# Top-32 attention and a hard-swish feed-forward: a shorter softmax chain, one reciprocal for two halves, and key/query transposes moved from TensorE to the DMA crossbar

## The chip, the cores and the metric

The kernel runs on one core of a Trainium2 chip, in one launch. The metric is the device time in microseconds. The kernel before takes 1581.81 us, the median of three runs (1580.72 to 1583.69). The execution that the profile shows took 1580.33 us and has a span of 1578.5 us from its first to its last instruction.

The core has five engines that run their own instruction streams, each strictly in the order in which the program wrote it, and wait for one another by semaphores: TensorE (PE in the profile, with its weight loads as PEld), VectorE (DVE), ScalarE (ACT), GpSimd (POOL) and SyncE (SP), which here issues the DMAs.

## What is computed

There are 8 batches with 8 heads, 576 queries and keys of 64 elements. In every row of 576 scores only the 32 largest are kept; their softmax weights the values. The result, 4608 tokens of 512, goes through a feed-forward layer of 2048 with a hard-swish gate.

```python
scores = scale * np.matmul(q, k.transpose(0, 1, 3, 2))
kth = np.partition(scores, -32, axis=-1)[..., -32:-31]
scores = np.where(scores >= kth, scores, -1e9)
attn = np.exp(scores - np.max(scores, axis=-1, keepdims=True))
attn = attn / (np.sum(attn, axis=-1, keepdims=True) + 1e-09)
x = np.matmul(attn, v)            # then (B,H,S,D) -> (B*S, H*D)
h = x @ w_in                      # 512 -> 2048
out = (h * np.clip(h + 3.0, 0.0, 6.0) / 6.0) @ w_out
```

## The kernel before

The words of the program: a **pair** is two heads of one batch, a **duo** is one tile of 128 queries of two pairs. In a duo each pair is one half (u = 0 or 1) with two rows of 576 scores per partition, one row for each head. The 64 queries that are left over from 576 = 4 x 128 + 64 make **leftover duos** (`rest`): both heads share the 128 partitions, and a half has one row only. There are 80 duos, 16 of them leftover.

The program is written as a sequence of **slots**, eight to a duo. In each slot VectorE gets one of the four rounds that find the 32 largest scores of a half:

```python
def top(self, u, r):                       # round r of half u
    ...
    for t in range(self.nt):               # nt = 2 rows, or 1 in a leftover duo
        nc.vector.max(self.m[u][:, t, 8*r : 8*r+8], self.cur[t])        # the 8 largest
    if r < TOP_K // 8 - 1:
        for t in range(self.nt):
            nc.vector.match_replace(wk, self.m[u][...], self.cur[t], LOWEST)
```

What follows for a half is a chain over the other engines:

```python
def shift(self, u):        # GpSimd: (32nd largest - largest) * scale
    nc.gpsimd.tensor_tensor(d[:, 0:nt], m[:, 0:nt, TOP_K-1], m[:, 0:nt, 0], ALU.subtract)
    nc.gpsimd.tensor_scalar_mul(d[:, 0:nt], d[:, 0:nt], scale)
def exp(self, u):          # ScalarE: Prelu, then Exp with the row's sum, then + EPS
    ... AF.Prelu, bias=m[:, t, TOP_K-1:TOP_K] ...
    ... AF.Exp, bias=self.less[u][:, t:t+1], accum_out=self.den[:, u, t:t+1] ...
    nc.scalar.activation(d, d, AF.Copy, bias=EPS)
def inverse(self, u):      # VectorE
    nc.vector.reciprocal(d, d)
def weights(self, u):      # GpSimd: times 1/sum, then the two 16-bit halves of each word apart
    ...
def flip(self, u):         # the DMA crossbar transposes the 16-bit halves
    nc.sync.dma_start_transpose(t16[:, 0:n, :], self.e16[u][:, 0 : n * P])
def join(self, u):         # halves together again: ScalarE for u = 0, GpSimd for u = 1
    ...
def values(self, dst):     # TensorE: weights times values;  place(): ScalarE copies the result
    ...
```

When each part is queued is a table of slots, counted from the duo's first slot; so 8 is the first slot of the next duo:

```python
usual = dict(
    shift0=3, exp0=4, inverse0=9, weights0=10, flip0=12, join0=15,
    shift1=7, exp1=8, inverse1=13, weights1=14, flip1=16, join1=19, values=22, place=23,
)
behind = dict(usual, values=25, place=26)      # second to next-to-last part of the run
```

After `place` of two full duos a **block** of 128 tokens goes to the feed-forward queue. A block has 16 **pieces**: eight make h = x @ w_in (a piece is 16 TensorE instructions of 128 columns), eight add h's gate times w_out into `acc` (4 instructions of 512 columns). Slots take about one piece each; a leftover duo's slots take half of that:

```python
due += ((left > 0) + (left >= 24) / 8 + (left >= 48) / 8) / (2 if u and u.rest else 1)
piece(int(due))
```

Keys and queries come as rows of 64 and are transposed on TensorE, nine instructions for a pair, and copied from PSUM by ScalarE:

```python
def transpose(self):
    ps = big()
    for j in range(2 * J + 1):
        rows = self.landed[:, j, :, :].rearrange("p h d -> p (h d)")
        nc.tensor.transpose(ps[:, j * P : (j + 1) * P], rows, ident[:])
    nc.scalar.copy(kq[:, 0:c0], ps[:, 0:c0])
    ...                                        # three smaller copies
```

The scores of the next duo are made in slot 1 (TensorE) and copied by ScalarE in the same slot. In the first duos the 64-bit weights are also turned into 32-bit words (`convert`: 32 chunks, ScalarE, GpSimd, then two VectorE instructions, lines 117 and 118, then GpSimd).

Of the kernel before, what the change touches and what calls it, by code (L numbers as in the profile page):

```python
# [29 lines left out]
def kernel(  # L30
# [65 lines left out]
    def convert(dst, src):  # L96

        st = kqpool.tile([P, 2 * WC], U32, tag="kq", name="st")
        nc.sync.dma_start(st[:], src)
        yield
        words = st[:].rearrange("p (n two) -> p n two", two=2)
        lo, hi = words[:, :, 0], words[:, :, 1]
        a = gpool.tile([P, WC], F32, tag="g", name="a")
        y = gpool.tile([P, WC], F32, tag="g", name="y")
        nc.scalar.activation(a[:], hi.bitcast(F32), AF.Abs)
        nc.gpsimd.tensor_scalar(a[:], a[:], HI_MOST, HI_LEAST, ALU.min, ALU.max)

        nc.scalar.activation(y[:], lo, AF.Copy, bias=2.0, scale=2.0**-51)
        yield

        au, yu = a[:].bitcast(U32), y[:].bitcast(U32)
        nc.vector.tensor_scalar(au, au, 3, None, ALU.logical_shift_left)  # L117
        nc.vector.scalar_tensor_tensor(  # L118
            out=yu, in0=hi, scalar=0x80000000, in1=yu,
            op0=ALU.bitwise_and, op1=ALU.bitwise_or,  # L120
        )
        yield
        nc.gpsimd.tensor_tensor(
            dst.bitcast(I32), a[:].bitcast(I32), y[:].bitcast(I32), ALU.add
        )
# [13 lines left out]
    class Pair:  # L139
# [6 lines left out]
        def load(self):  # L146
            h0 = 2 * self.hp
            t = self.landed = kqpool.tile([P, 2 * J + 1, 2, D], F32, tag="kq", name="landed")
            for i, src in enumerate((k, q)):
                for hh in range(2):  # L150
                    nc.sync.dma_start(
                        t[:, i * J : (i + 1) * J, hh, :],
                        src[self.b, h0 + hh, 0:JP, :].rearrange("(p j) d -> p j d", j=J),
                    )
                nc.sync.dma_start(
                    t[i * R : (i + 1) * R, 2 * J, :, :],
                    src[self.b, h0 : h0 + 2, JP:S, :].rearrange("h s d -> s h d"),
                )
# [12 lines left out]
        def transpose(self):  # L171
            kq = kqpool.tile([P, JP + S], F32, tag="kq", name="kq")
            self.kT, self.qT = kq[:, 0:JP], kq[:, JP : JP + S]
            ps = big()
            for j in range(2 * J + 1):
                rows = self.landed[:, j, :, :].rearrange("p h d -> p (h d)")
                nc.tensor.transpose(ps[:, j * P : (j + 1) * P], rows, ident[:])  # L177
            c0 = 2 * JP
            nc.scalar.copy(kq[:, 0:c0], ps[:, 0:c0])
            nc.scalar.copy(kq[:, c0 : c0 + R], ps[:, c0 + R : c0 + 2 * R])  # L180
            for hh in range(2):
                d = slice(hh * D, (hh + 1) * D)
                nc.scalar.copy(self.kr[d, hh, :], ps[d, c0 : c0 + R])

    class Duo:
# [14 lines left out]
        def scores(self, us=(0, 1)):  # L200

            if us[0] == 0:
                self.sc = scpool.tile([P, 2, 2 * (S + R)], F32, tag="sc", name="sc")
                self.den = mpool.tile([P, 2, 2], F32, tag="den", name="den")
            sc, nu = self.sc[:, us[0] : us[-1] + 1, :], len(us)
            ps = big()
# [4 lines left out]
            if self.rest:  # L211
                for i, u in enumerate(us):
                    pr = self.pairs[u]
                    for d in heads:
                        nc.tensor.matmul(banks[d, i, :], pr.qT[d, qs], pr.kT[d, :])
                    for hh, d in enumerate(heads):
                        nc.tensor.matmul(left[d, i * R : (i + 1) * R], pr.qT[d, qs], pr.kr[d, hh, :])
                nc.gpsimd.memset(sc[:, :, S : S + R], 0.0)
                nc.scalar.copy(sc[:, :, 0:JP], banks[:, 0:nu, :])
                nc.scalar.copy(  # L220
                    sc[:, :, JP:S], left[:, 0 : nu * R].rearrange("p (u r) -> p u r", r=R)
                )
                return
# [5 lines left out]
            for i, u in enumerate(us):  # L229
                pr = self.pairs[u]  # L230
                for hh, d in enumerate(heads):
                    nc.tensor.matmul(banks[:, 2 * i + hh, :], pr.qT[d, qs], pr.kT[d, :])  # L232
            nc.scalar.copy(  # L233
# [25 lines left out]
        def shift(self, u):  # L259

            nt, m = self.nt, self.m[u]
            d = self.less[u] = mpool.tile([P, 2], F32, tag="shift", name="shift")
            nc.gpsimd.tensor_tensor(
                d[:, 0:nt], m[:, 0:nt, TOP_K - 1], m[:, 0:nt, 0], ALU.subtract
            )
            nc.gpsimd.tensor_scalar_mul(d[:, 0:nt], d[:, 0:nt], scale)  # L266

        def exp(self, u):
# [7 lines left out]
            for t in range(nt):  # L276
                row = self.row(u, t)
                nc.scalar.activation(  # L278
                    row, row, AF.Exp, bias=self.less[u][:, t : t + 1], scale=-scale / FLAT,
                    accum_out=self.den[:, u, t : t + 1],  # L280
                )
            d = self.den[:, u, 0:nt]
            nc.scalar.activation(d, d, AF.Copy, bias=EPS)

        def inverse(self, u):
            d = self.den[:, u, 0 : self.nt]
            nc.vector.reciprocal(d, d)  # L287
# [64 lines left out]
    def feed_forward(xT, rows):  # L352
# [6 lines left out]
        for f0 in range(0, NFC, nf):  # L359
# [12 lines left out]
            g = gpool.tile([P, 512], F32, tag="g", name="g")  # L372
            nc.scalar.activation(g[:], h[:], AF.Relu, bias=three[:], scale=1.0)  # L373
            hs = hpool.tile([P, 512], F32, tag="h", name="hs")
            nc.scalar.copy(hs[:], h[:])
            gs.append(g)

            def gate(g=g, hs=hs):
                nc.gpsimd.tensor_scalar(g[:], g[:], 6.0, 0.0, ALU.min, ALU.max)  # L379
                nc.gpsimd.tensor_tensor(g[:], g[:], hs[:], ALU.mult)  # L380

            yield gate
        acc = ps_w.tile([P, DM], F32, tag="w", name="acc")
        for f in range(NFC):
# [7 lines left out]
            if f % 2 == 1:  # L392
                if f == NFC - 1:
                    o = opool.tile([P, DM], F32, tag="o", name="o")
                    nc.scalar.mul(o[:], acc[:], 1.0 / 6.0)  # L395
                    for p0, p1, dst in rows:
                        nc.sync.dma_start(dst, o[p0:p1, :])
                yield None

# [5 lines left out]
    for b in range(B):  # L405
        halves = [pairs[b][0:2], pairs[b][2:4]]
        for qt in range(J):
# [3 lines left out]
            if qt == (0 if b == B - 1 else J - 1) and not 2 < b < B - 1:  # L411
# [11 lines left out]
    gates = []  # L423

    def piece(count=1):
        nonlocal left
        for _ in range(count):
            while todo:
                try:
                    gates.append(next(todo[0]))  # L430
                    left -= 1
                    break
                except StopIteration:
                    todo.pop(0)
            else:
                gates.append(None)
            if len(gates) > 2:
                gate = gates.pop(0)
                if gate:
                    gate()  # L440
# [45 lines left out]
    def land(count=1):  # L486

        for _ in range(min(count, len(chunks))):
            c = convert(*chunks.pop(0))
# [20 lines left out]
    def pair_at(m, first):  # L510
# [5 lines left out]
    first[0].load()  # L516
    land(2)
    first[1].load()
    first[0].transpose()
    convert_step()  # L520
    duos[0].scores((0,))
    convert_step()
    first[2].load()
    convert_step()
    first[1].transpose()
    duos[0].scores((1,))
    land()


# [3 lines left out]
        shift0=3, exp0=4, inverse0=9, weights0=10, flip0=12, join0=15,  # L533
        shift1=7, exp1=8, inverse1=13, weights1=14, flip1=16, join1=19, values=22, place=23,
    )

    behind = dict(usual, values=25, place=26)
    early = dict(
        shift0=3, exp0=3, inverse0=4, weights0=4, flip0=5, join0=8,
        shift1=7, exp1=7, inverse1=8, weights1=8, flip1=9, join1=12, values=12, place=13,  # L540
    )
    soon = dict(
        shift0=3, exp0=3, inverse0=5, weights0=5, flip0=7, join0=10,
        shift1=7, exp1=7, inverse1=9, weights1=9, flip1=11, join1=14, values=16, place=17,
    )
    queued = {}
    for m in range(ND):
        for part, at in (early if m < 2 else soon if m >= ND - 2 else behind if per_batch <= m < ND - 4 else usual).items():
            queued.setdefault(8 * m + at, []).append((m, part))

    def parts(slot, late=None):

        for m, part in sorted(queued.get(slot, []), key=lambda x: x[1][:-1] != "shift"):
            if late is not None and (part[:-1] in ("inverse", "weights")) != late:
# [3 lines left out]
            elif part == "place":  # L558
                place(m)
            else:  # L560
# [3 lines left out]
    for m in range(ND + 3):  # L564
        u = duos[m] if m < ND else None
        for i in range(8):
# [7 lines left out]
            if m == 0 and i in (1, 2):  # L574
                first[i + 1].transpose()
            if i == (4 if m == 0 else 1) and m + 1 < ND:
                duos[m + 1].scores()
            if m < 4:
# [6 lines left out]
            if i == 0:  # L585
                p = pair_at(m, 4)
# [5 lines left out]
            if i == 5:  # L592
                p = pair_at(m, 5)
                if p:
                    p.transpose()

            due += ((left > 0) + (left >= 24) / 8 + (left >= 48) / 8) / (2 if u and u.rest else 1)
            piece(int(due))
            due -= int(due)
    while todo:  # L600
        piece()
    piece(2)
# [33 lines left out]
```

## Time and profile before

| | busy, us | share of the span |
|---|---|---|
| PE (matmuls) | 1456.9 | 92% |
| PEld (weight loads) | 1039.0 | 66% |
| DVE | 1466.8 | 93% |
| ACT | 1096.3 | 69% |
| POOL | 1144.5 | 73% |
| DMA queue | | 43.5% of 16 engines |

A row of the groups reads: line, engine, operation, what it writes and reads, shapes, count, then busy time and mean of one, then the idle time of that engine just before such instructions and what ended it. Matmuls are pipelined, so a mean can be longer than the distance from one to the next. In the chain that ended last, each row is a start, a length and what ran; it is followed back from the last instruction. A row of the waits is: engine and line, what it waited for, total us, times, and the longest.

### The profile page before, as it was taken

The numbers are of one execution on the slowest core, as the hardware profiler recorded it, in microseconds if no ns is written. First come the engines' busy times: TensorE is split into PE (matmuls) and PEld (weight loads), VectorE is DVE, ScalarE is ACT, GpSimd is POOL, SyncE is SP. The second block draws the span as 40 slices with busy tenths as digits, with TensorE's granted clock in tenths as the row PEclk, the third lists the DMA queues.
The fourth block names the chain that finished last, engine by engine and source line by source line (L and its number), as shares of the span: only waits on it lengthen the run. The fifth ranks groups of instructions, "written<-read, shape, count | busy, mean of one in ns | idle before, by whom it ended". The sixth has DMA issues, their size and how long they took to land.

```text
span 1578.5 us, 28787 instructions
## 1 busy us (share of the span) xinstructions
PE 1456.9 (92%) x10272; PEld 1039.0 (66%) x10272; DVE 1466.8 (93%) x3105; ACT 1096.3 (69%) x1865; POOL 1144.5 (73%) x1264
## 2 busy tenths in 40 slices
PE   5256799979999999998999999999999999999899
PEld 3153566567767777666777777776777767677675
DVE  6999999999999999999999999999999999999700
ACT  6675777777777777777776786777766787777621
POOL 4868687777867777867687777867687777767841
PEclk9568999989999999999999999999999999999999
DMA  8652543444344543545254543446244443533410
GB/s 236 159 181 45 113 83 81 94 91 97 76 90 89 101 83 76 101 85 119 55 106 76 97 89 82 93 93 116 57 96 87 98 88 74 103 65 68 83 22 14
DMA packets 450319, 144.49 MB, mean 92 GB/s; under 512 B 433280, under 2 KB 441472, under 8 KB 450176
## 3 DMA queue, kind: packets, MB, share of 16 engines
q1 hardware_dynamic: 450176, 142.65, 43.5%
q8 instruction: 81, 1.33, 0.3%
q14 instruction: 62, 0.51, 0.1%
HBM read 45.09 MB, written 9.44 MB: 35 GB/s over the span
## 4 chain that ended last, share of the span: by engine, by line
DVE 51%; PE 35%; POOL 5%; issue 3%; ACT 3%; DMA 1%; SPq 1%; POOLq 0%; ACTq 0%; DVEq 0%
DVE m L250 26%; DVE wk L254 22%; PE h L365 14%; PE acc L385 13%; PE pv L338 4%; PE big L232 3%; POOL e L306 1%; DVE y L118 1%; POOL sc L297 1%; DMA t<-e 1%; POOL eT L318 1%; DVE a L117 1%; PE big L177 1%; ACT sc L278 1%; ACT eT L318 1%
## 5 line engine op out<-in xcount | busy, mean ns | idle before, releaser
L250 DVE MAX8 m<-wk 128x8 f32<-128x576 f32 x864 | 613.1, 746 | 2.2
L385 PE MATMUL acc<-w_out,g 128*128 128x512 f32 x1152 | 516.9, 600 | 14.1 <-POOL g L380 14.1
L365 PE MATMUL h<-xT,w_in 128*128 128x128 f32 x4096 | 485.5, 279 | 17.3 <-ACT xT L348 17.3
L365 PEld LDWEIGHTS h<-xT,w_in 128*128 128x128 f32 x4096 | 475.0, 195 | 39.5 <-issue 18.2
L254 DVE MATCH_REPLACE8 wk<-m,wk 128x576 f32<-128x576 f32 x576 | 423.7, 742 | 0.0
L385 PEld LDWEIGHTS acc<-w_out,g 128*128 128x128 f32 x1152 | 213.6, 191 | 260.4 <-issue 238.6
L297 POOL TENSOR_SCALAR sc<-sc,den 128x576 f32<-128x576 f32 x288 | 213.8, 753 | 229.9 <-DVE den L287 222.7
L306 POOL COPY e<-sc 128x2304 uint16<-128x2304 uint16 (+1 forms) x192 | 320.3, 1678 | 10.2
L278 ACT ACTIVATE sc<-sc,shift 128x576 f32<-128x576 f32 x288 | 220.4, 769 | 40.5 <-POOL shift L266 37.7
L318 ACT COPY eT<-t 128x2304 uint16<-128x2304 uint16 (+1 forms) x82 | 215.9, 2632 | 37.9 <-DMA t<-e 35.3
L273 ACT ACTIVATE sc<-sc,m 128x576 f32<-128x576 f32 x288 | 210.1, 777 | 46.2 <-DVE m L250 46.0
L338 PE MATMUL pv<-eT,vm 128*64 128x128 f32 (+1 forms) x2560 | 164.0, 273 | 57.9 <-ACT eT L318 45.8
L254 DVE MATCH_REPLACE8 wk<-m,sc 128x576 f32<-128x576 f32 x288 | 211.8, 742 | 0.0
L318 POOL COPY eT<-t 128x2304 uint16<-128x2304 uint16 (+1 forms) x78 | 203.8, 2613 | 6.9 <-DMA t<-e 6.5
L338 PEld LDWEIGHTS pv<-eT,vm 128*64 128x64 f32 x2560 | 135.2, 141 | 109.3 <-ACT eT L318 49.7
L250 DVE MAX8 m<-sc 128x8 f32<-128x576 f32 x288 | 203.3, 742 | 2.4 <-ACT sc L236 2.4
L373 ACT ACTIVATE g<-h,three 128x512 f32<-128x512 f32 x144 | 98.5, 684 | 150.0 <-PE h L365 140.6
L380 POOL TENSOR_TENSOR g<-g,hs 128x512 f32<-128x512 f32 x144 | 185.0, 1285 | 12.1 <-POOL g L379 0.2
L233 ACT COPY sc<-big 128x2048 f32<-128x2048 f32 (+1 forms) x65 | 119.3, 1836 | 26.1 <-PE big L232 26.0
L232 PE MATMUL big<-kq 64*128 64x512 f32 x512 | 136.4, 653 | 0.0
L379 POOL TENSOR_SCALAR g<-g 128x512 f32<-128x512 f32 x144 | 89.2, 620 | 62.6 <-ACT g L373 52.4
L395 ACT ACTIVATE o<-acc 128x512 f32<-128x512 f32 x36 | 21.4, 595 | 106.6 <-PE acc L385 106.6
(47 smaller groups left out, 1113.1 us busy)
## 6 DMA issues: line engine op xcount, KB each, us to landing
landed<-in_k_dram SPq DMA_DIRECT2D x64, 128.0 KB, 3.0
landed<-in_q_dram SPq DMA_DIRECT2D x64, 128.0 KB, 3.0
st<-in_moe_w_in_dram SPq DMA_DIRECT2D x16, 512.0 KB, 5.1
vm<-in_v_dram SPq DMA_DIRECT2D x64, 128.0 KB, 2.3
st<-in_moe_w_out_dram SPq DMA_DIRECT2D x16, 512.0 KB, 6.6
out_dram<-o SPq DMA_DIRECT2D x32, 256.0 KB, 2.4
t<-e SPq DMA_TRANSPOSE x160, 4.6
landed<-in_k_dram SPq DMA_DIRECT2D x32, 32.0 KB, 2.8
```

The costliest lines, as they stand in the source:

```text
L232: nc.tensor.matmul(banks[:, 2 * i + hh, :], pr.qT[d, qs], pr.kT[d, :])
L250: nc.vector.max(self.m[u][:, t, 8 * r : 8 * r + 8], self.cur[t])
L254: nc.vector.match_replace(wk, self.m[u][:, t, 8 * r : 8 * r + 8], self.cur[t], LOWEST)
L273: nc.scalar.activation(row, row, AF.Prelu, bias=m[:, t, TOP_K - 1 : TOP_K], scale=-1.0, alpha=FLAT)
L278: nc.scalar.activation(row, row, AF.Exp, bias=self.less[u][:, t : t + 1], scale=-scale / FLAT, accum_out=self.den[:, u, t : t + 1],)
L297: nc.gpsimd.tensor_scalar(row, row, self.den[:, u, t : t + 1], 1.0, ALU.mult, ALU.mult)
L306: nc.gpsimd.tensor_copy(halves[:, :, to : to + c1 - c0], words)
L318: copy(eT[:, 0 : self.nb, :] .rearrange("p c q -> p (c q)") .bitcast(U16) .rearrange("p (x h) -> p h x", h=2), self.t16[u][:, 0 : 2 * self ...
L338: nc.tensor.matmul(pv[hh * D : (hh + 1) * D, u * w : (u + 1) * w], pr.vm[:, hh, c, :] if c < J else pr.vr[:, hh, :], rhs, start=(c == 0), ...
L365: nc.tensor.matmul(h[:, (f - f0) * P : (f - f0 + 1) * P], w_in[:, i, f * P : (f + 1) * P], xT[:, i, :], start=(i == 0), stop=(i == NHP - 1),)
L380: nc.gpsimd.tensor_tensor(g[:], g[:], hs[:], ALU.mult)
L385: nc.tensor.matmul(acc[:], gs[f // nf][:, f % nf * P : (f % nf + 1) * P], w_out[:, f, :], start=(f == 0), stop=(f == NFC - 1),)
```

## The change

Five things change.

- **Keys and queries of batches 1 to 7** no longer go through TensorE. GpSimd splits each 32-bit word into two 16-bit halves (`split`), a crossbar DMA transposes them (`flip`), ScalarE joins them (`join`). The first batch is transposed as before.
- **The chain of a duo is shorter.** shift moves from GpSimd to ScalarE as two or three small activations; both halves share one "+ EPS" (`settle`) and one reciprocal; weights, flip, join, values and place stand earlier.
- **ScalarE's reads of h and of acc** are queued one piece later than the matmuls that make them, and the copy of the next duo's scores stands in slot 4 while its matmuls stay in slot 1, so that ScalarE meets work that is done.
- **At the start** the first pair's q is loaded through ScalarE's DMA queue, and for the first 16 weight chunks one intermediate (`y`) lies in PSUM.
- **In the last batch** the leftover duos stand after the second query tile instead of the first, and the last duo has its own table.

The diff, cut to its core:

```diff
+        y = ps_w.tile(...) if early else gpool.tile(...)          # convert
+        ys = gpool.tile([P, WC], F32, tag="g", name="ys") if early else y
         nc.vector.scalar_tensor_tensor(
-            out=yu, in0=hi, scalar=0x80000000, in1=yu, ...
+            out=ys[:].bitcast(U32), in0=hi, scalar=0x80000000, in1=yu, ...
...
+        def split(self):
+            self.e16 = kqpool.tile([P, 2 * (2 * J + 1) * P], U16, tag="kq", name="e16")
+            nc.gpsimd.tensor_copy(...)                  # 128 x 2304 halves
+        def flip(self):
+            nc.sync.dma_start_transpose(self.t16[:], self.e16[:])
+        def join(self):
+            copy(kq[:, 0:c0], halves[:, :, 0:c0])       # ScalarE, 1024 words
+            copy(kq[:, c0 : c0 + R], halves[:, :, c0 + R : c0 + 2 * R])
+            ...                                         # two more of 64 words
...
         def shift(self, u):
-            nc.gpsimd.tensor_tensor(... ALU.subtract)
-            nc.gpsimd.tensor_scalar_mul(...)
+            nc.scalar.activation(d[:, 1, 0:nt], m[:, 0:nt, 0], AF.Copy, scale=-scale)
+            for t in range(nt):
+                nc.scalar.activation(d[:, 0, t : t + 1], m[:, t, TOP_K - 1 : TOP_K],
+                    AF.Identity, bias=d[:, 1, t : t + 1], scale=scale)
...
-        def inverse(self, u):
-            d = self.den[:, u, 0 : self.nt]
+        def inverse(self, us):
+            d = self.den[:, us[0] : us[-1] + 1, 0 : self.nt]
             nc.vector.reciprocal(d, d)
+        def settle(self, us):
+            nc.scalar.activation(d, d, AF.Copy, bias=EPS)
...
     usual = dict(
-        shift0=3, exp0=4, inverse0=9, weights0=10, flip0=12, join0=15,
-        shift1=7, exp1=8, inverse1=13, weights1=14, flip1=16, join1=19, values=22, place=23,
+        shift0=3, exp0=4, shift1=7, exp1=8, settle01=8, inverse01=10, weights0=10, weights1=11,
+        flip0=12, flip1=13, join0=15, join1=16, values=17, place=18,
     )
-    behind = dict(usual, values=25, place=26)
...
+    last = dict(
+        shift0=3, exp0=3, settle0=3, inverse0=5, weights0=5, flip0=7, join0=10,
+        shift1=7, exp1=7, settle1=7, inverse1=8, weights1=8, flip1=9, join1=11, values=11, place=11,
     )
...
+            if i == 4 and m + 1 < ND:
+                duos[m + 1].store()
...
-            if i == 5:
-                p = pair_at(m, 5)
-                if p:
-                    p.transpose()
+            for at, first_at, part in ((2, 4, "split"), (5, 4, "flip"), (2, 5, "join")):
+                p = pair_at(m, first_at) if i == at else None
+                if p:
+                    getattr(p, part)()
...
+            if not left:
+                piece()
```

Within a slot, shifts are queued first; what is left of the slot's parts follows in the order of the duos. So in slot 7 of a duo ScalarE gets shift1 of that duo and then join0 of the duo before it.

## The prediction

> **What bounds the kernel now.** I read the engine totals first, then the 40 slices, then VectorE's own waits.
>
> ```profile
> PE 1456.9 (92%) x10272; PEld 1039.0 (66%) x10272; DVE 1466.8 (93%) x3105; ACT 1096.3 (69%) x1865; POOL 1144.5 (73%) x1264
> DVE  6999999999999999999999999999999999999700
> ...
> DVE a L117 <- POOL a L109: 13.3, 2, 10.0
> DVE den L287 <- ACT den L283: 9.3, 4, 6.7
> DVE m L250 <- ACT sc L236: 2.4, 2, 1.7
> ```
>
> TensorE and VectorE look equally full. They are not. VectorE is back to back: its last MAX8 ends at 1491.3 us (timeline of the end), it was busy 1466.6 us until then, so it idled 25 us, 12 of them before its first MAX8 at 13.59. Its waits inside the body come to about 6 us. TensorE's 92% is not throughput: the h matmuls are listed at a mean of 279 ns, but the chain has 64 of them in 7.14 us, 112 ns each; acc is listed at 600 ns and runs 16 in 6.87 us, 429 ns. One feed-forward block (128 h, 32 acc) is thus 14.3 + 13.7 = 28.1 us, and one batch needs 4.5 blocks (126) + 8 values of 2.33 (19) + scores (about 22) + 4 transposes of about 1.3 (5) = 172 us, against 178 us of VectorE. So **VectorE sets the pace up to 1491**; then comes a tail of 87 us in which it does nothing:
>
> ```profile
> 1495.72 2.24 PE pv L338 x20
> 1497.96 4.46 PE h L365 x32
> 1502.42 10.30 PE acc L385 x24
> 1512.72 2.33 PE pv L338 x40
> 1515.05 3.63 PE acc L385 x8
> 1518.68 14.29 PE h L365 x128
> 1532.97 13.74 PE acc L385 x32
> 1546.71 14.29 PE h L365 x128
> 1561.00 13.75 PE acc L385 x32
> ```
>
> The reader should count here: a piece is 16 h or 4 acc matmuls, so these are 2+6+2+8+8+8+8 = 42 pieces of 28.1 / 16 = 1.76 us, 74 us. They stand after the last VectorE slot in program order, so TensorE is not late: the tail is a matter of the static order.
>
> **What the Trainium skill says.** "Perfetto Trace Analysis", Identifying the Most-Contended Engine, calls matmul busy time a poor measure of headroom; the 279 against 112 ns above agrees. "DMA: Bandwidth & Descriptors", DMA Transpose (X-bar), says that the plain transpose is issued by Sync or Scalar only and that two transposing streams must not be in flight together; here all 160 are on Sync (4.6 us to landing), and the 28 new ones join that stream. "VectorE: DVE Perf Modes", the section on two Vector instructions with no wait between them, describes a second SBUF read interface shared with GpSimd; line 118, with two SBUF inputs, takes 0.68 us undisturbed and up to 1.75 us here, which fits. "Perfetto Trace Analysis", Optimizing Scalar/DVE Operations, gives about 93 ns of access overhead for Scalar on SBUF and a profiled latency of about twice that; the tiny line 283 takes 203 ns.
>
> **The change, part by part.**
>
> *Transposes off TensorE.* 28 of 32 pairs, 9 transposes each, about 1.2 to 1.4 us with the break around them: 28 x 1.3 = 36 us of TensorE. TensorE is not the bound, so I give this nothing. The price: GpSimd 28 splits x 2.10 (row e, 2304 words) = +59 us, less the shift (69 us in four rows) = about -10; ScalarE 28 joins of about 3.3 us (2.8 us for 2304 words, scaled to 2048, plus three small ones) less the PSUM copies 1.01 + 0.22 + 0.42 = 1.65: +46 us.
>
> *Shift on ScalarE.* Three activations of about 0.2 us for a full half, two for a leftover half: 128 x 0.6 + 32 x 0.4 = +90 us. Half the den activations go: -16 us. ScalarE ends near 1096 + 46 + 90 - 16 = 1216 us, 77%. It still has room as a total.
>
> *One reciprocal a duo.* 80 fewer. A reciprocal is listed at 153 ns, but it overlaps its neighbours: from one MATCH_REPLACE8 to the round after it is 2.11 us with it (862.01 to 864.12) and 2.05 us without (868.94 to 870.99). So 79 x 0.06 = **-5 us**.
>
> *Start.* q on the second queue: three issues of 0.63 us no longer stand behind those of k: **-2 us** before the first MAX8. y in PSUM for 16 weight chunks: line 118 from a mean of 0.94 towards 0.68: 16 x 0.26 = 4, I take **-3 us**.
>
> *Tail.* I follow the count of pieces left, slot by slot, through the loop. Before, 26 are queued at VectorE's end and the last block adds 16: 42. After, the second-last block is placed five slots earlier, so 19 + 16 = 35. But the last values stand only three pieces behind VectorE's end, and their chain is longer: shift 0.8, then the other half's join 2.8, exp and settle 3.2, reciprocal 0.2, weights 3.6, transpose 5, join 2.8 = 18.4 us; values 1.2, 32 pieces 56.2, write 3.5: 79 us against 87. **-8 us**.
>
> *The wait I expect instead.* Gains so far: 5 + 2 + 3 + 8 = 18 us, plus 2 us for a wait at 1371 that changes its form. Now the order in ScalarE's stream. The second half's shift stands in slot 7. It cannot start until the duo's last MAX8 ends; call that zero. Behind it, in the same slot, stands join0 of the duo before (sorted behind shift), and exp1 and settle come in slot 8. Before, shift was on GpSimd, so join0 could run ahead. So the sum is ready at 0.2 + 0.6 + 2.8 + 2.95 + 0.2, plus a read of h (1.26 us) that lies between in about 3 of 10 cases: **about 7.1 us**. The common reciprocal now stands in slot 10, after three rounds of the next duo. Three rounds of a full duo take 2.79 + 2 x 2.77 = 8.3 us: just enough. Three rounds of a leftover duo (64 queries, one row) take 3 x 1.63 = **4.9 us**: VectorE waits about 2.3 us. Before, the second half's reciprocal stood in slot 13, so it had 8 us or more. The kernel before shows this wait once, where a transpose held the join:
>
> ```profile
> 1366.68 2.79 ACT L318 COPY eT<-t 128x2304 uint16<-128x2304 uint16 x1 [3.65 <-DMA t<-e]
> 1369.33 0.77 ACT L273 ACTIVATE sc<-sc,m 128x576 f32<-128x576 f32 x1
> 1370.19 0.78 ACT L278 ACTIVATE sc<-sc,shift 128x576 f32<-128x576 f32 x1
> 1370.88 0.19 ACT L278 ACTIVATION_READ_ACCUMULATOR sc<-sc,shift 128x1 f32 x1
> 1371.09 0.20 ACT L283 ACTIVATE den<-den 128x1 f32<-128x1 f32 x1
> ```
>
> (one core, leftover duo; join, then exp, then den, and VectorE's reciprocal at 1371.33 after 1.43 us idle.) There are 16 leftover duos. Twelve follow a full duo: 12 x 2.5 = 30 us. Four follow another leftover: exp1 is half as long, but join0 there must wait for a transpose whose weights now start late; I take 2 us each, 8 us. In seven the pair's 3.3 us join stands in slot 2, ahead of the store of the next scores, and costs perhaps 0.5 us more. **About +40 us.**
>
> Sum: 1581.8 - 20 + 40 = 1602.
>
> **Rivals.** (1) *The wait does not come.* If ScalarE reaches exp1 earlier than I think, only the gains stand: 1581.8 - 20 = 1562. For it: ScalarE's 140.6 us of waiting for h vanish when reads are a slot late, and the change is plainly tuned with tight slots. Against it: the reads' waits are not in the 7.1 us at all. (2) *TensorE was the bound from 733 to 1211 us*, where the chain of waits runs through it. Then 28 x 1.3 = 36 us come on top and the time is near 1545. Against it: VectorE is at 49.66 of 50 us or more in nearly every stretch of that window, so the time cannot shrink there without VectorE shrinking. (3) *ScalarE becomes the bound everywhere.* A full duo with a pair's join needs 15.4 + 3.3 = 18.7 of 19.4 us in my sum; a few more waits for transposes would then make the reciprocal late in full duos too, whose slack is only 8.3 - 7.1 = 1.2 us. 1 us in each of 64 duos would give 1660. Against it: the other six duos of ten have 4 us spare and catch up. (4) *The transposes hold up the Sync queue.* 28 more of 2.7 us issue is 75 us in 1580 on a queue that mostly waits; I expect nothing of it.
>
> **Range and chances.** I give the wait in leftover duos three in four (1602, less a little since waits may absorb each other, about 1600 +- 12), rival 1 nearly all the rest (1566 +- 8), and a small part to the others. The mean is 1594; eight times in ten between 1563 and 1613. Faster by over 2% means under 1550: 0.05. Slower by over 2% means over 1613.4: 0.10. Within: 0.85.
>
> **What would show it.** VectorE's list of waits: the reciprocal waiting for ScalarE's den goes from 9.3 us in 4 waits to 30 to 45 us in some 16, all in leftover duos, 2 to 3 us each. VectorE's last MAX8 ends near 1519 instead of 1491. Between that and the end, 79 us and 35 pieces. First MAX8 near 11.6. ScalarE's busy time near 1216, GpSimd's near 1134, line 118 of the early chunks near 0.7 us. The TensorE total falls by some 30 us with no stretch of VectorE shorter for it. I am wrong if VectorE's wait for den stays under 10 us, if it shows in full duos as well, or if the tail is as long as before.

## The result, and the profile after

The changed kernel takes 1633.43 us (median of four runs, 1630.23 to 1636.65) against 1581.5 us for the kernel before: a ratio of 1.0326, 95% interval 1.0298 to 1.0354. It is slower by 52 us, where 1594 was predicted, with 1613 as the upper end.

The first lines are from the page of the changed kernel: the engine totals, and VectorE's busy tenths in 40 slices.

```profile
PE 1462.3 (90%) x10020; PEld 1031.0 (63%) x10020; DVE 1460.6 (90%) x3028; ACT 1210.7 (74%) x2236; POOL 1133.0 (70%) x972
...
DVE  6998989999899988998999989998999989999900
```

VectorE does 6 us less work than before (1460.6 against 1466.8), but where its row had nines without a break it now has eights, all through the run: it waits. ScalarE has 114 us more, GpSimd 12 us less, both close to what was worked out ahead. TensorE's total did not fall: 1462.3 us against 1456.9, with 252 instructions fewer. Its mean granted clock was 0.945 in this profile and 0.963 before. That does not explain the loss: of two runs below, e14 has 0.966 and is 17 us slower than the kernel before, e18 has 0.957 and is 8 us faster.

Where the waiting sits can be read from VectorE's timeline: the start of each duo's first MAX8, and the difference to the next duo's. A wait before a duo's first MAX8 thus counts to the duo before it. Summed by kind of duo (us):

| | before | after | difference |
|---|---|---|---|
| up to the first MAX8 | 13.6 | 13.5 | -0.1 |
| first four duos (weights converted beside them) | 130.5 | 127.6 | -2.9 |
| 59 full duos | 1144.7 | 1150.2 | +5.5 |
| 16 leftover duos | 182.8 | 237.1 | +54.3 |
| last duo | 19.6 | 19.4 | -0.2 |
| tail behind the last MAX8 | 87.3 | 81.2 | -6.1 |
| span | 1578.5 | 1629.0 | +50.5 |

Nearly all of the loss lies in the 16 leftover duos: 11.4 us each before, 14.8 us now. Who waits for whom has changed as well. The next lines are from the waits of the changed kernel over all engines.

```profile
POOL eT L372 <- DMA t<-e: 195.3, 57, 9.2
ACT xT L402 <- PE pv L392: 123.7, 46, 6.8
...
DVE den L337 <- ACT den L341: 54.9, 28, 6.1
...
PE pv L392 <- POOL eT L372: 47.9, 27, 4.2
...
DVE m L296 <- ACT sc L282: 15.0, 9, 4.3
```

And the same waits in the kernel before:

```profile
ACT xT L348 <- PE pv L338: 23.7, 14, 8.8
...
PE pv L338 <- POOL eT L318: 12.1, 5, 4.4
...
POOL eT L318 <- DMA t<-e: 6.5, 3, 4.9
```

Read from the DMA on: GpSimd's join waits for the crossbar (6.5 us before, 195.3 now; ScalarE's join waits less, 35.3 before and 14.9 now), TensorE's values wait for that join (12.1, now 47.9), ScalarE's place waits for the values (23.7, now 123.7), and VectorE waits for ScalarE: for den 9.3 us, now 54.9, and for scores 2.4, now 17.2 (the 15.0 above and 2.2 in a row of its own, L275). The timeline of the changed kernel shows one such chain link by link, in a leftover duo. Each line is a start, a length, engine, line, operation, and in brackets the idle time before it and what ended it.

```profile
1316.43 2.75 POOL L372 COPY eT<-t 128x2304 uint16<-128x2304 uint16 x1 [4.86 <-DMA t<-e]
...
1319.23 1.98 PE L392 MATMUL pv<-eT,vm 128*64 128x128 f32 x16 [3.94 <-POOL eT L372]
...
1321.68 0.37 ACT L402 COPY xT<-pv 128x256 f32<-128x256 f32 x1 [4.24 <-PE pv L392]
1321.95 2.69 ACT L215 COPY kq<-t 128x2048 uint16<-128x2048 uint16 x2
...
1325.64 1.84 ACT L279 COPY sc<-big 128x2048 f32<-128x2048 f32 x1
1327.39 0.37 ACT L282 COPY sc<-big 128x256 f32<-128x256 f32 x1
1327.79 1.42 DVE L296 MAX8 m<-sc 128x8 f32<-128x576 f32 x2 [4.29 <-ACT sc L282]
```

The crossbar's 4.86 us become TensorE's 3.94, ScalarE's 4.24 and at last VectorE's 4.29. Every stream is in order, so a wait in one is handed on to whatever is queued behind it. Between place and the copy of the scores stands also the join of a pair (L215, 1321.95 to 1325.18, some 3.2 us); both together make the scores late.

### The profile page after: what moved, and what is told of

It reads as the page before. It is cut to its first block, busy times and chain, and to the rows that moved or that the text cites. A ratio compares the mean times of both kernels' runs of the same rounds, so it can differ in the third digit from the quotient of the medians.

```text
span 1629.0 us, 28236 instructions
## 1 busy us (share of the span) xinstructions
PE 1462.3 (90%) x10020; PEld 1031.0 (63%) x10020; DVE 1460.6 (90%) x3028; ACT 1210.7 (74%) x2236; POOL 1133.0 (70%) x972
## 4 chain that ended last, share of the span: by engine, by line
PE 24%; DVE 23%; ACT 11%; POOL 9%; DMA 3%; issue 3%; POOLq 0%; SPq 0%; ACTq 0%; DVEq 0%
DVE m L296 13%; DVE wk L300 10%; PE acc L443 9%; PE h L419 9%; DMA t<-e 3%; PE pv L392 3%; POOL eT L372 3%; POOL e L360 2%; ACT eT L372 2%; ACT sc L329 2%; ACT sc L324 2%; POOL sc L351 2%; PE big L262 2%; ACT kq L215 1%; POOL g L436 1%
## 5 line engine op out<-in xcount | busy, mean ns | idle before, releaser
L443 PE MATMUL acc<-w_out,g 128*128 128x512 f32 x1152 | 526.7, 610 | 18.1 <-POOL g L436 18.0
L419 PEld LDWEIGHTS h<-xT,w_in 128*128 128x128 f32 x4096 | 477.5, 196 | 22.5 <-issue 16.3
L443 PEld LDWEIGHTS acc<-w_out,g 128*128 128x128 f32 x1152 | 218.0, 195 | 277.7 <-issue 245.9
L372 POOL COPY eT<-t 128x2304 uint16<-128x2304 uint16 (+1 forms) x78 | 203.1, 2604 | 205.8 <-DMA t<-e 195.3
L392 PE MATMUL pv<-eT,vm 128*64 128x128 f32 (+1 forms) x2560 | 177.6, 287 | 118.1 <-ACT eT L372 53.0
L392 PEld LDWEIGHTS pv<-eT,vm 128*64 128x64 f32 x2560 | 143.7, 148 | 178.2 <-ACT eT L372 70.0
L372 ACT COPY eT<-t 128x2304 uint16<-128x2304 uint16 (+1 forms) x82 | 213.5, 2604 | 15.0 <-DMA t<-e 14.9
L296 DVE MAX8 m<-sc 128x8 f32<-128x576 f32 x288 | 205.3, 755 | 17.2 <-ACT sc L282 15.0
L436 POOL TENSOR_TENSOR g<-g,hs 128x512 f32<-128x512 f32 x144 | 184.1, 1279 | 12.1
L311 ACT ACTIVATE shift<-m,shift 128x1 f32<-128x1 f32 x288 | 75.0, 290 | 61.1 <-DVE m L296 56.8
```

The lines of the kernel that those rows point to most:

```text
L296: nc.vector.max(self.m[u][:, t, 8 * r : 8 * r + 8], self.cur[t])
L372: copy(eT[:, 0 : self.nb, :] .rearrange("p c q -> p (c q)") .bitcast(U16) .rearrange("p (x h) -> p h x", h=2), self.t16[u][:, 0 : 2 * self ...
L392: nc.tensor.matmul(pv[hh * D : (hh + 1) * D, u * w : (u + 1) * w], pr.vm[:, hh, c, :] if c < J else pr.vr[:, hh, :], rhs, start=(c == 0), ...
L419: nc.tensor.matmul(h[:, (f - f0) * P : (f - f0 + 1) * P], w_in[:, i, f * P : (f + 1) * P], xT[:, i, :], start=(i == 0), stop=(i == NHP - 1),)
L443: nc.tensor.matmul(acc[:], gs[f // nf][:, f % nf * P : (f % nf + 1) * P], w_out[:, f, :], start=(f == 0), stop=(f == NFC - 1),)
```

## The experiments

Three theories. **A**: the order in slot 7; join0 stands between the last MAX8 and exp1, so the sum is late for the shared reciprocal (the prediction's). **B**: the chain is too short; joins, values and place stand where the crossbar has not yet delivered, and the engines that wait there hold up what is queued behind. **C**: ScalarE is too full with shifts and the pairs' joins. For theory B it matters how far the parts moved. The second half's weights, flip and join stand three slots earlier than before, while those of the first half keep their slots. For 66 of the 80 duos values and place stood in slots 25 and 26 (the table `behind`), so in the changed kernel they come eight slots earlier, not five. All times are medians; 1581 us is the kernel before in each comparison. The columns "leftover" and "full" are the sums over 16 and 59 duos as in the table above, from each run's profile.

| run | time, us | leftover | full | tail |
|---|---|---|---|---|
| before | 1581 | 182.8 | 1144.7 | 87.3 |
| after | 1633.4 | 237.1 | 1150.2 | 81.2 |
| e1 join0 ahead of shift1 | 1637.2 | 235.9 | 1157.1 | 79.6 |
| e2 values and place later | 1611.4 | 217.3 | 1142.5 | 89.8 |
| e3 both | 1605.7 | 212.9 | 1143.2 | 88.0 |
| e4 both, pair's join in slot 5 | 1611.2 | 215.3 | 1147.1 | 90.0 |
| e5 long chain | 1601.5 | 210.4 | 1141.7 | 93.6 |
| e6 long chain, TensorE transposes | 1609.1 | 217.1 | 1141.4 | 93.5 |
| e7 TensorE transposes | 1614.3 | 224.0 | 1145.8 | 82.4 |
| e8 shift on GpSimd | 1632.5 | 236.3 | 1153.1 | 80.4 |
| e9 long chain, scores copied in slot 1 | 1596.8 | 207.0 | 1141.4 | 92.4 |
| e10 e9 with faster pieces and more | 1628.4 | 240.2 | 1149.2 | 80.3 |
| e11 e10 with TensorE transposes | 1626.0 | 238.6 | 1147.1 | 79.9 |
| e12 e9 with reads at once | 1599.3 | 203.3 | 1141.5 | 94.2 |
| e13 short chain alone | 1630.1 | 216.4 | 1166.8 | 82.3 |
| e14 one reciprocal, long chain, alone | 1598.4 | 202.0 | 1141.4 | 95.3 |
| e15 e14 with crossbar | 1606.6 | 210.9 | 1142.2 | 93.9 |
| e16 e14 with shift on ScalarE | 1607.0 | 211.3 | 1141.5 | 93.8 |
| e17 start and last batch only | 1575.9 | 180.3 | 1144.8 | 87.3 |
| e18 the change with the old chain | 1573.4 | 186.6 | 1144.8 | 84.1 |

### Order, distance, or both

**e1**: join0 ahead of shift1 in ScalarE's stream.

```diff
-        ... key=lambda x: x[1][:-1] != "shift"
+        ... key=lambda x: {"join": 0, "shift": 1}.get(x[1][:-1], 2)
```

> Edit: in a slot, ScalarE's join0 of the duo before is queued ahead of shift1 instead of behind it; nothing else. Theory A (the order in slot 7: join0, 2.8 us, stands between the last MAX8 and exp1): the sum is ready about 4.3 us after the last MAX8 instead of 7.1, before the 4.9 us of three rounds of a leftover duo. VectorE's wait for den falls from 49 us in the body (54.9 with the tail) to under 12, the 16 leftover duos lose some 30 us of their extra 57, VectorE ends near 1515, time near 1598. Theory B (a short chain: values and place come too early, and place blocks ScalarE): den waits fall by less than 15 us, the waits for scores stay at 15 us, time near 1620. Theory C (ScalarE is just too full): den waits barely move, time within 8 us of 1633.

Measured: 1637.2 us, ratio 1.0357 (1.034 to 1.0374): nothing gained. VectorE's waits in e1:

```profile
DVE den L337 <- ACT den L341: 54.0, 25, 5.1
DVE m L296 <- ACT sc L282: 19.1, 11, 5.6
```

The den waits are as long as before the edit. In four leftover duos the first half did fall to 5.6 or 5.7 us, as theory A has it (before the edit 7.0 or 7.1 us in all four). But ScalarE's own wait for the crossbar in front of join0 rose from 14.9 to 33.0 us, and other duos lost what these won. Taken as the cause of the loss, A falls.

**e2**: values and place three slots later, for all but the last four duos.

```diff
+    later = dict(usual, values=20, place=21)
```

> Edit: values and place three slots later (20 and 21 instead of 17 and 18) for all but the last four duos; nothing else. Theory A: the wait for den in leftover duos stays near 40 us; time 1622 to 1635. Theory B: ScalarE's 123.7 us of waiting for pv nearly vanish, so do VectorE's 15 us of waiting for scores, and the 10 us in full duos; time near 1610. Theory C: no change, within 8 us of 1633.

Measured: 1611.4 us, ratio 1.019 (1.0175 to 1.0205). From the waits of e2:

```profile
DVE den L337 <- ACT den L341: 32.8, 13, 7.4
...
ACT xT L402 <- PE pv L392: 13.5, 3, 7.9
...
DVE den L337 <- ACT shift L309: 7.9, 4, 3.0
...
DVE den L337 <- POOL eT L372: 4.1, 2, 2.8
...
DVE m L296 <- ACT sc L282: 2.4, 3, 1.7
```

ScalarE's wait for the values falls from 123.7 to 13.5 us, VectorE's for scores from 17.2 to 2.4, the full duos are near their floor again (1142.5; some 1141.3 where nothing waits), and 22 us come back. GpSimd's wait for the crossbar is still 189 us, so it was not that wait which cost, but its being handed on. What stays is the wait for den, 44.8 us in three rows: 7.4 in the tail and 35.4 in leftover duos, where the changed kernel has 40.4. So the handed-on wait makes the scores late, and den late in full duos (8.2 us, now 1.9), but hardly den in leftover duos.

**e3** and **e4**: both edits, then the join of a pair behind the copy of the scores as well.

```diff
-            for at, first_at, part in (..., (2, 5, "join")):
+            for at, first_at, part in (..., (5, 5, "join")):
```

> Edit: both edits, join0 ahead of shift1 and values and place three slots later. If A and B are two separate waits their gains add: VectorE's waits for den and scores together under 10 us, leftover duos near 11.5 us each, VectorE ends near 1486, time near 1570. If one hides the other, the time is within 5 us of the better of the two single edits. C: above 1610.

> Edit: as both edits, and the join of a pair (3.4 us of ScalarE) in slot 5, behind the copy of the next scores, instead of slot 2. If the pair's join holds up the copy of the scores in leftover duos: 3 to 8 us less than with both edits alone, waits for scores near 0. If not: within 3 us of it.

Measured: 1605.7 and 1611.2 us. With values and place out of the way the order of join0 is worth 6 us, far from adding up to 1570. Moving the pair's join costs 5.5 us: it then stands in front of the next shift1 and exp1.

### The load

**e7** undoes the crossbar alone, **e8** the shift alone, both in the short chain.

```diff
-            for at, first_at, part in ((2, 4, "split"), (5, 4, "flip"), (2, 5, "join")):   # e7
+            if i == 5: p.transpose(); p.store()
-            nc.scalar.activation(...) x 2 or 3                                              # e8: shift
+            nc.gpsimd.tensor_tensor(... ALU.subtract); nc.gpsimd.tensor_scalar_mul(...)
```

> Edit: the changed kernel (short chain) with keys and queries of all batches transposed on TensorE again. Theory B (the chain is too short whatever the load): within 12 us of 1633. Theory C (ScalarE's load): ScalarE's busy time falls by some 46 us, the waits for den and scores by half or more, time near 1605.

> Edit: the changed kernel with shift on GpSimd again, as before the change; nothing else. If the move of shift (90 us of small ScalarE instructions, and ScalarE held until the last MAX8) makes the den late: den waits fall by 20 us or more, time near 1605. If the too short chain does: GpSimd's own queue, which waits for transposes, delays the shift as well, and the time is 1625 to 1650.

Measured: 1614.3 and 1632.5 us. Neither theory had e7 right. Without the crossbar's pairs the short chain costs 19 us less; VectorE's wait for scores falls from 17.2 to 2.4 us, for den (all its rows) only from 54.9 to 53.0. ScalarE's wait for the values hardly falls (123.7, now 114.4). So in the short chain the pairs' joins on ScalarE do add to the loss: the scores are late only where place's wait and a pair's join come together. The shift on ScalarE changes nothing there.

**e13** turns it around: the short chain without the crossbar, without the shift on ScalarE, without late reads or the late copy of scores.

```diff
-            if len(reads) > 1:          # reads one piece late
+            if len(reads) > 0:          # at once; and e7, e8, and store() behind scores() in slot 1
```

> Edit: the changed kernel with the crossbar, the shift on ScalarE, the late reads and the late copy of the scores all undone; what stays is the short chain with one reciprocal, the start and the order of the last batch. Theory B/E (the short chain makes TensorE and ScalarE wait for joins that wait for the crossbar, and TensorE has no slack to make it up): near 1615, TensorE's waits for pv's inputs over 60 us more than in the kernel before. Theory C (ScalarE's load from crossbar and shift): near 1580.

Measured: 1630.1 us, ratio 1.0308 (1.0292 to 1.0323). **The short chain alone costs as much as the whole change.** From its waits:

```profile
POOL eT L367 <- DMA t<-e: 99.7, 43, 6.3
...
DVE den L332 <- ACT den L336: 67.9, 35, 5.5
...
PE pv L387 <- POOL eT L367: 53.2, 21, 5.4
```

The same links are there: join behind the crossbar, values behind the join. ScalarE waits longer at several places: for h 168.9 us (140.6 in the kernel before, which reads h at once as well), for its own join's crossbar 54.8 (35.3), for the values 48.4 (23.7), for scores 41.8 (26.0). VectorE meets this through den. Here two fifths of VectorE's loss lie in full duos (1166.8 against 1144.7). Theory C falls as the cause. The parts do not add: without crossbar and late reads the loss is as large as with both.

### The long chain

**e5**: from the reciprocal on the distances that the old table gave the second half, for both halves, and still one reciprocal a duo. values and place stand in 22 and 23, which for most duos is still three slots earlier than before. **e6**: the same without the crossbar.

```diff
+    later = dict(usual, inverse01=13, weights0=13, weights1=14, flip0=15, flip1=16,
+                 join0=18, join1=19, values=22, place=23)
```

> Edit: the changed kernel with the old distances in the chain and still one reciprocal for both halves: inverse01 13, weights 13 and 14, flip 15 and 16, join 18 and 19, values 22, place 23 (all but the last two duos). Theory B+ (the shared reciprocal stands too early for a leftover duo, values and place too early for the crossbar; nothing else in the change costs): VectorE's waits for den in the body fall from 49 to under 5 us, for scores from 17 to under 3, VectorE ends near 1482, and with a tail of 85 to 90 us the time is about 1570. Theory C (ScalarE too full with shifts and joins): the waits only move, time above 1600.

> Edit: as e5_long_chain, and keys and queries of all batches transposed on TensorE again (slot 5, as before). If the crossbar's splits and joins are hidden beside VectorE once the chain is long, and TensorE's transposes are too: within 6 us of e5. If TensorE is the bound in the middle: 20 to 35 us more than e5. If the 46 us of extra ScalarE work cost: 10 us or more less than e5.

Measured: 1601.5 and 1609.1 us. In e5 the wait for den in the body is gone (9.9 us, 8.3 of it after the last MAX8, none in a leftover duo), as it should be if the shared reciprocal in slot 10 stood too early for leftover duos. But 31.6 us of waiting for scores have come instead:

```profile
DVE m L296 <- ACT sc L282: 18.4, 9, 4.0
DVE m L296 <- ACT sc L275: 13.2, 3, 6.8
```

The likely reason is that the first half's join (18 slots on, so slot 2 of the duo after the next) is now queued ahead of the copy of the scores in slot 4, and a leftover duo is short for both. The crossbar here saves 8 us: its sign depends on the chain around it.

**e9**: the copy of the scores in slot 1 again. **e12**: the reads at once as well.

```diff
-            if i == 4 and m + 1 < ND:
-                duos[m + 1].store()
+                duos[m + 1].store()     # right behind scores(), slot 1
```

> Edit: as e5_long_chain, and the copy of the next duo's scores in slot 1 again, right behind its matmuls, instead of slot 4. Theory D (in a leftover duo, half as long, slot 4 puts the copy behind ScalarE's join and the pair's join, so it comes too late): VectorE's 31 us of waiting for scores in e5 fall under 6, VectorE ends near 1482 instead of 1508, time about 1575. Theory C (ScalarE too full): the waits come back elsewhere, time above 1592.

> Edit: as e9, and ScalarE's reads of h and acc in the slot of their matmuls, as before the change. If the late reads save ScalarE's waiting for TensorE: ScalarE's wait for h rises by 50 us or more, and the time by 3 to 15 us. If VectorE's pace hides it: within 3 us of e9.

Measured: 1596.8 and 1599.3 us. The copy in slot 1 is worth 5 us, not 26: VectorE's wait for scores falls from 31.6 to 14.3 us, but its wait for den rises from 9.9 to 22.3, and ScalarE waits 144.7 us for TensorE's scores (26.0 in the kernel before). The late reads are worth 2.5 us. The expectation for the wait for h (50 us more) was met: 37.9 us became 99.6.

**e10** and **e11** were meant as the best version: e9 with the pair's join in slot 5, the short chain for the last four duos only, and pieces given out faster.

```diff
-            due += ((left > 0) + (left >= 24) / 8 + (left >= 48) / 8) / ...
+            due += ((left > 0) + (left >= 8) / 8 + (left >= 24) / 8) / ...
```

> Edit: as e9, and the pair's join in slot 5; the short chain for the last four duos only; and a block's pieces a little faster (a ninth piece in eight slots from 8 queued pieces on, not from 24), which leaves 18 + 16 pieces behind VectorE's end instead of 24 + 16. If TensorE has room for it in the middle: the tail falls from 93 us to about 78, time about 1560, 20 us under the kernel before. If TensorE has none: VectorE waits for scores again, time above 1575.

> Edit: as e10, with all keys and queries transposed on TensorE. If the crossbar is worth TensorE's 36 us once nothing waits: 5 to 20 us more than e10, in TensorE's lag and in the tail. If it is hidden: within 5 us of e10.

Measured: 1628.4 and 1626.0 us. The tail did shrink, to 80.3 us, but the leftover duos grew by 33 us; from e10's waits:

```profile
ACT sc L279 <- PE big L262: 146.2, 54, 5.4
...
DVE den L337 <- ACT den L341: 50.9, 19, 7.6
DVE m L296 <- ACT sc L282: 20.1, 10, 4.0
```

The first of these rows was 144.7 us in e9 already; it is the wait for den that grew, from 22.3 us. Of the three edits the pair's join is not it: e11 has no such joins and is as slow. The last four duos are full ones at the end, and the loss is in leftover duos. So the ninth piece is left as the cause, though it was not run alone. That TensorE has no room for it is not shown: e11 puts some 36 us of transposes (the prediction's estimate) back on TensorE and is 2 us faster than e10.

### One reciprocal, and the change without the short chain

**e14**: one reciprocal and the long chain on the kernel before (with the start and the last batch of the change). **e15** adds the crossbar, **e16** the shift on ScalarE; e12 has both. **e17** is e14 with the old tables and a reciprocal for each half.

```diff
+    usual = dict(shift0=3, exp0=4, settle0=4, inverse0=9, weights0=10, flip0=12, join0=15,      # e17
+        shift1=7, exp1=8, settle1=8, inverse1=13, weights1=14, flip1=16, join1=19, values=22, place=23)
+    behind = dict(usual, values=25, place=26)               # 66 of the 80 duos
```

> Edit: as e13 with the long chain of e5: against the kernel before one reciprocal a duo, the first half's weights three slots later, the start and the order of the last batch. If one reciprocal is free and saves its 5 to 8 us: 1570 to 1582. If sharing it costs (the first half's chain starts later and its buffers are held longer): above 1590.

> Edit: as e14 with keys and queries of batches 1 to 7 through the crossbar. If TensorE has no slack, the 36 us taken from it come through: 10 us or more under e14. If ScalarE's 46 and GpSimd's 59 us more cost as much: within 5 us of e14 or above it.

> Edit: as e14 with shift on ScalarE. If ScalarE held until the last MAX8 (and 90 us of small instructions) delays its copies of scores: 8 to 20 us over e14. If it is hidden: within 4 us of e14.

> Edit: as e14, with the table of the kernel before (a reciprocal for each half, inverse0 9, weights0 10 and so on, values 22 or 25): the kernel before, but for the start, the order of the last batch and the flush of reads. If sharing the reciprocal costs the 17 us (both halves' weights stand together and the first half's join falls into the next duo's slot 2): 1575 to 1584. If the start or the last batch costs them: 1592 or more.

Measured: 1598.4, 1606.6, 1607.0 and 1575.9 us. e14 costs 22 us more than e17: 21.7 in leftover duos (202.0 against 180.3) and 8 in the tail, less some 7 won in the first four and the full duos. The two differ in three things: the shared reciprocal, the first half's weights, flip and join three slots later, and values and place, which in e14 stand three slots earlier for 66 duos. The full duos do gain what was expected of the sharing: 1144.8 to 1141.4, 0.06 us a duo. One row of e14's waits, 32.4 us in e17, points at the weights:

```profile
ACT sc L324 <- POOL shift L312: 127.2, 51, 11.3
```

ScalarE's exp waits for GpSimd's shift, and both halves' weights, 7 us of GpSimd's work close together, now stand in front of that shift. Of the 21.7 us, 17.1 are VectorE's waits for den in nine leftover duos. In five of them (10.5 us) ScalarE had come from such a wait for shift, in the other four (6.6 us) from a wait for h. The three differences were not run apart. Each of crossbar and shift adds 8 us to e14, both together 1 us (e12).

e17 itself is faster than the kernel before, ratio 0.9965 (0.9953 to 0.9978): the start and the last batch (with the empty piece that is queued when none is left) are worth 5 us.

**e18** is the whole change, with the old table and the copy of the scores in slot 1.

> Edit: the changed kernel with the table of the kernel before (a reciprocal for each half) and the copy of the scores in slot 1; crossbar, shift on ScalarE and late reads stay. If these parts are nearly neutral by themselves: 1575 to 1592. If TensorE's 36 us come through once the chain is long: under 1572, faster than the kernel before. If ScalarE's load counts: above 1595.

Measured: **1573.4 us, ratio 0.995 (0.9936 to 0.9963)**, the fastest of all, 60 us under the changed kernel. From its waits:

```profile
POOL eT L372 <- DMA t<-e: 19.5, 10, 4.0
...
DVE den L337 <- ACT den L341: 11.0, 9, 3.7
...
DVE m L296 <- ACT sc L282: 1.7, 1, 1.7
```

The links of the chain are short again. Against e17, crossbar, shift and late reads together bring 2.6 us; the two intervals overlap, so that is hardly more than nothing.

## Why the prediction was right or wrong

**Right.** VectorE sets the pace, and the crossbar, the shift and the late reads together hardly move the time (e18 beside e17), though TensorE is relieved of its transposes. The wait takes the form foretold: the reciprocal waits for den, above all in leftover duos, where all 16 have such a wait. e5, where the shared reciprocal and what follows it stand later, has none there, which fits the reason that the prediction gave: a slot too early for a leftover duo. ScalarE's busy time (1210.7 against 1216), GpSimd's (1133.0 against 1134), the reciprocal's worth (3.4 us over 59 full duos, so some 4.5 over all, against 5) and the tail (81.2 against 79) came out as worked out. y in PSUM did so in part: line 118, now 124, fell to 0.675 us in the sixteen early chunks, and the four first duos are 2.9 us shorter, against 3. But the 0.94 was the mean of all 32 chunks. The early ones had 1.00, and the other sixteen rose from 0.89 to 1.07, so that the line as a whole gained 2.3 us.

**Wrong: the term "about +40 us" in "The wait I expect instead".** It had three parts, and the profile of the changed kernel gives each:

| | foretold, us | measured, us |
|---|---|---|
| den in leftover duos | 12 x 2.5 + 4 x 2 = 38 | 31.9 + 8.6 = 40.4 |
| scores late at the end of a leftover duo | 7 x 0.5 = 3.5 | 15.5 (9 waits) |
| full duos | nothing | 8.2 (den, 10 waits) |

Of the 54.9 us of waiting for den another 6.1 lie in the tail, and of the 17.2 for scores 1.7 in the first duo. The second and third part are the step that failed: 20 of the 29 us by which this profile (1630.9 us) exceeds 1602. A wait for den in full duos was also one of the signs named for being wrong. Both parts come from a link that the prediction left out: place waits for values, values for join1, join1 for the crossbar. e2 moves values and place alone and takes the two from 15.5 to 0.7 us and from 8.2 to 1.9. For the scores the pair's join has to stand in the way as well, the 0.5 us of the prediction: without it (e7) they are on time, too. The tables were there to see it. The second half's weights cannot end before about 8.3 + 7.1 = 15.4 us after the duo's end, and the crossbar needs 4.6 us to landing, so the halves are there after 20.0 us. join1 stands eight slots after the duo's end: 19.3 us on if the next duo is full, but only about 11.4 if it is a leftover. In the changed kernel these weights end at a median of 17.9 us where a full duo follows a full one, and 16.3 where a leftover duo follows.

The first part has the right size, but by luck. The 7.1 us started ScalarE free at the last MAX8, and often it was not. In the first leftover duo, from the timeline of ScalarE in the changed kernel:

```profile
219.67 0.68 ACT L429 ACTIVATE g<-h,three 128x512 f32<-128x512 f32 x1
...
221.75 0.23 ACT L309 ACTIVATE shift<-m 128x2 f32<-128x2 f32 x1
...
222.40 2.75 ACT L372 COPY eT<-t 128x2304 uint16<-128x2304 uint16 x1
...
228.01 0.20 ACT L341 ACTIVATE den<-den 128x4 f32<-128x4 f32 x1
```

The last MAX8 had ended at 218.9, but the shift starts at 221.75, behind two reads of h; den starts 9.1 us after that MAX8, and VectorE waits 4.57 us. Where ScalarE was free (five of the sixteen, the duo with the chain shown above among them), den started 5.8 or 5.9 us after it and VectorE waited 1.33 to 1.35 us. The mean of the twelve that follow a full duo was 2.7 us, which is the 2.5 I took, but for the wrong reason: e1 takes the 2.8 us of join0 out, four of these five duos no longer wait, and the total hardly changes (54.9, now 54.0 us).

**Wrong: the start.** The first MAX8 stands at 13.54, not 11.6. q did land earlier, but the transposes start at 5.78 us, waiting for k, and the copy from PSUM begins at 7.96 as it did before (8.01).

**Wrong: TensorE's total.** It was to fall by some 30 us and rose by 5.4. The transposes' rows did fall, from 41.5 to 8.7 us, but the matmuls of the values were listed at a mean of 302 ns instead of 285 (pv<-eT,vm), and those of acc at 610 instead of 600. The cause stays open.

**The rivals.** Rival 1 (the wait does not come) and rival 2 (TensorE the bound, 36 us gained) did not happen. With the old chain put back, the crossbar brings, together with the shift and the late reads, 2.6 us (e18 less e17). Rival 3 (the reciprocal late in full duos too) is there, at 8 us instead of 60. Rival 4 put its finger on the crossbar, but on its queue; what matters is when its input is ready, for without the 28 transposes (e7) GpSimd waits 214.1 us for the crossbar instead of 195.3.

**Open**: how much of e14's 22 us is the sharing, how much the later first half and how much the earlier values and place, what a ninth piece by itself costs (e10), and why the parts combine as they do (the crossbar costs 19 us in the short chain, saves 8 in e5, costs 8 in e15).

## What to carry to other kernels

In a schedule written as fixed slots for in-order engines, check for each moved step when its input can be ready at the earliest, by adding up the durations from the last producer: a step queued too early does not start sooner, it blocks its engine and hands the wait on. Do it for the shortest kind of iteration, since the slots shrink there and the chain does not. And when a change has several parts, run it once with the schedule put back: here the parts around it were worth 8 us together, and the shorter chain with its shared reciprocal and the later copy of the scores cost 60.

## What the runs showed of the hardware that was not expected

Two kinds of tiny ScalarE activations were listed with different lengths in the changed kernel: those of the shift with a bias per partition (L311, 128x1) at a mean of 290 ns, those without one (L309, 128x2) at 210 ns. They differ in their function as well (Identity and Copy), and no run here separates the two. The copy from the crossbar's halves into words took 2.52 us for 128x2048 halves of 16 bits on ScalarE, and the two smaller joins of 64 partitions 336 ns each, where the PSUM copies of the same words took 209 in the kernel before.

A VectorE instruction at line 118 reads two operands in SBUF and took between 0.68 and 1.75 us in the early chunks; with one operand in PSUM (line 124) all 16 took 0.67 or 0.68 us.
